# An S4D convolution and a token MLP on one core: the last four pieces of the inverse transform taken from SBUF, with a small selection table and moved loads

## The chip, the cores and the metric

One core of a Trainium2 chip. The metric is the device time of one execution in microseconds. The kernel before took 704.68 us (median of 3 runs, 703.97 to 706.22).

## What is computed

An adaLN block over x of 2048 tokens and 448 channels: a layer norm with modulation, a long convolution with an S4D kernel (done as an FFT of 4096 points), a second layer norm, and an MLP across the token axis.

```python
mod = (_silu(c) @ w_mod).reshape(c.shape[0], 6, 1, -1)
sa, ca, ga, sb, cb, gb = (mod[:, k] for k in range(6))
h = _layernorm(x, axis=-1) * (1 + ca) + sa
x = x + ga * _A_ref(h, ...)        # y = irfft(rfft(h) * rfft(K)) + h * D_skip, K from the S4D parameters
h = _layernorm(x, axis=-1) * (1 + cb) + sb
x = x + gb * _B_ref(h, ...)        # layernorm over channels, then across tokens: (gelu(h^T w1 + b1) w2 + b2)^T
```

## The kernel before

The order of the instructions of PE (TensorE), DVE (VectorE), ACT (ScalarE) and POOL (GpSimd) is that of the code; the transfers stand in SP's queue in the order of the code too, and a transfer that waits holds up all that are behind it in that queue. SP waits ahead of each transfer for the one issued eight before it, as there are eight counters in turn.

The work has three parts. The first generates the convolution's kernel and the transforms of kernel and input. The second multiplies the two spectra and transforms back. It goes by 32 *pieces*: piece n is a pair of frequency rows (p = n mod 16) of one half of the channels (c = n div 16, DC = 224 channels each). Pieces 0 to 15 run beside the first part; pieces 16 to 31 run in the loop `for m in range(NP, 2 * NP + 2, 2)` (NP = 16), two in each round. A piece is

- `pc_load`: the input's spectrum `u` from DRAM (224 KB)
- `pc_s2`: eight matmuls `kx` on PE for the kernel's spectrum
- `pc_mul`: two products `zx`, `zy` on DVE, then two sums `z` on the engines that it is given (POOL, or DVE for the last piece)
- `pc_inv`: eight matmuls `vv`
- `pc_out`: two copies on ACT into `vt` (four buffers), and a transfer of it (224 KB) to `v_d` in DRAM

In round m PE does `kx` of m and m + 1, and then `vv` of m - 2 and m - 1.

The third part reads the rows of `v_d` back by token blocks r (16 blocks of 128 tokens; `ln_load`, 448 KB), finishes the inverse transform with the table `ft` (`ln_y`), adds x (`x_pair` loads two blocks of it, 2 x 224 KB), applies the layer norms (`y_sum`, `ln_mod`, `ln_out`) and feeds the MLP, whose weights a `WeightStream` loads (`wst.load`, 448 KB each time), rounds on ACT (`whi`) and corrects on DVE (`wlo`). The MLP's matmuls write `acc` and later `o`.

Blocks 0 and 1 don't wait for all of `v_d`. Their channel half 0 is loaded early (`ln_first`); half 1 is loaded for the pieces that are already out (`ln_second`), and the products of the latest pieces come from their `vt` in SBUF (`fresh_vt`): the table `fl` selects from such a `vt` the rows of block r with their factors, in matmuls of 128 x 128 by 128 x 224 (`ln_direct`), and `ln_main` adds the loaded rows. In the kernel before, these are the last two pieces, `fl` is a full table of 512 KB from DRAM, and `ln_main` takes 112 rows.

Of the kernel before, what the change touches and what calls it, by code (L numbers as in the profile page):

```python
# [11 lines left out]
F32 = mybir.dt.float32  # L12
# [9 lines left out]
L, D, N, F = 2048, 448, 256, 1792  # L22
P = 128
# [9 lines left out]
NP = 16  # L33
# [6 lines left out]
def dft_tables():  # L40
    n1 = np.arange(32)
    k1 = np.arange(32)
    n2 = np.arange(64)
    k2 = np.arange(64)
    nn = 4096
    t = {}
    w = 2 * np.pi * np.outer(n1, k1) / 64
    w1 = np.zeros((2, 32, 32))
    w1[0] = np.cos(w)
    w1[1] = -np.sin(w)  # L50
    w1[0, :, 0] = 1
    w1[1, :, 0] = (-1.0) ** n1
    wc = np.zeros((4, 32, 2, 4, 32))
    for g in range(4):
        for c in range(2):
            wc[g, :, c, g, :] = w1[c]
    wu = np.zeros((2, 2, 32, 32, 2, 2))
    for a in range(2):
        wu[:, a, ..., a] = w1.transpose(1, 2, 0)
    t["WU"] = wu.reshape(P, P)  # L60

    t["WC"] = wc.reshape(P, 2, 2, 2, 32).swapaxes(3, 4).reshape(P, 2 * P)
    s = np.zeros((2, 64, 32, 2, 64))
    i1 = np.zeros((2, 64, 32, 2, 64))
    i2 = np.zeros((2, 64, 32, 2, 64))

    def inverse(rows, cols, k, m, ang):
        a = np.cos(ang) * 2 / nn
        b = np.sin(ang) * 2 / nn
        i1[0, rows, k, m[0]] = a  # L70
        i1[1, rows, k, m[0]] = -b
        i2[1, rows, k, m[0]] = -a
        i2[0, rows, k, m[0]] = -b
        if len(m) > 1:
            i1[0, rows, k, m[1]] = b
            i1[1, rows, k, m[1]] = a
            i2[1, rows, k, m[1]] = -b
            i2[0, rows, k, m[1]] = a

    for k in range(1, 32):  # L80
        ang = 2 * np.pi * np.outer(n2, k + 64 * k2) / nn
        s[0, :, k, 0] = np.cos(ang)
        s[1, :, k, 0] = np.sin(ang)
        s[0, :, k, 1] = -np.sin(ang)
        s[1, :, k, 1] = np.cos(ang)
        inverse(slice(None), None, k, (0, 1), ang.T)


    for q in range(32):
        ang = 2 * np.pi * n2 * (32 + 64 * q) / nn  # L90
        s[1, :, 0, 0, q] = np.cos(ang)
        s[1, :, 0, 1, q] = -np.sin(ang)
        inverse(q, None, 0, (1,), ang)
    for q in range(33, 64):
        ang = 2 * np.pi * n2 * (64 * (q - 32)) / nn
        s[0, :, 0, 0, q] = np.cos(ang)
        s[0, :, 0, 1, q] = -np.sin(ang)
        inverse(q, None, 0, (0,), ang)
    s[0, :, 0, 0, 32] = 1
    s[0, :, 0, 1, 32] = (-1.0) ** n2  # L100
    i1[0, 32, 0, 0] = 1 / nn
    i2[1, 32, 0, 0] = (-1.0) ** n2 / nn
    s2 = s.reshape(P, 32 * P)

    su = s.swapaxes(3, 4).reshape(2, 64, 32, P)
    t["S2"] = su.reshape(2, 2, 2, 16, 32 * P).swapaxes(1, 2).reshape(P, 32 * P)

    one = np.einsum("cnk,cqkm->km", w1, su)
    t["SV"] = one[ones_k1()].T

    order = lambda a: a.reshape(P, 32, 2, 2, 2, 16).swapaxes(3, 4).reshape(2, 64, 32, P)
    v1, v2 = order(i1), order(i2)
    pairs = v1.reshape(2, 64, NP, 2, P).transpose(3, 1, 2, 0, 4).reshape(P, NP, 2 * P)
    t["SI"] = np.concatenate([s2.reshape(P, NP, 2 * P), pairs], 2).reshape(P, NP * 4 * P)
    t0 = np.zeros((P, 2, P))
    t0[32, 0] = v1[0, 32, 0] + v2[1, 32, 0]
    t0[:, 1] = pairs[:, 0, P:]
    t["T0"] = t0.reshape(P, 2 * P)
    ft = np.zeros((32, 2, 2, 32, 2))
    w = 2 * np.pi * np.outer(k1, n1) / 64  # L120
    f0 = np.cos(w)
    f1 = -np.sin(w)
    f0[0] = 1
    f1[0] = (-1.0) ** n1
    for h in range(2):
        ft[:, 0, h, :, h] = f0
        ft[:, 1, h, :, h] = f1
    t["FT"] = ft.reshape(P, 64)

    fl = np.zeros((2, 2, 2, 16, 2, 4, 2, 32, 2))  # L130
    for r in range(2):
        for g in range(2):
            fl[:, :, g, r, r, :, g] = ft[28:].transpose(1, 2, 0, 3, 4)
    t["FL"] = fl.reshape(P, 8 * P)


    te = np.zeros((3, 64, 16, 32))
    tg = np.zeros((3, 16, 4, 16, 32))
    n = np.arange(32)
    for d in range(16):  # L140
        te[0, 2 * d : 2 * d + 2, d] = 2 * n + 1
        te[2, 2 * d : 2 * d + 2, d] = -n
        tg[0, d, 0:2, d] = n
        tg[0, d, 2:4, d] = 1
        tg[2, d, 0:2, d] = -64 * n
        tg[2, d, 2:4, d] = 1
    tg = tg.reshape(3, 16, 2, 2, 512).swapaxes(1, 2)
    tt = np.concatenate([te.reshape(3, 64, 512), tg.reshape(3, 64, 512)], 1)
    tt[1] = -tt[0]
    t["TT"] = tt.reshape(3, P, 512)  # L150
    return {k: np.ascontiguousarray(v.astype(np.float32)) for k, v in t.items()}
# [74 lines left out]
def tile_adaln_s4d_mixer(ctx, tc, i, out):  # L226
    nc = tc.nc
# [19 lines left out]
    with ExitStack() as es:  # L247
# [514 lines left out]
        def pc_tables(n):  # L762

            real, h = pt[n][0], P // 2
            if n == NP:
                pt[n] = real, t0[:, 1]
                return
            imag = fp.tile([P, P], F32, tag="bt", name="bt", bufs=3)
            S.activation(imag[:, 0:h], real[:, h:P], AF.Copy, scale=-1.0)
            S.copy(imag[:, h:P], real[:, 0:h])  # L770
            pt[n] = real, imag
# [36 lines left out]
        def pc_out(n):  # L808
            c, p = divmod(n, NP)
            vt = swp.tile([P, 2, DC], F32, tag="vt", name="vt", bufs=4) if c else fp.tile([P, 2, DC], F32, tag="vt", name="vt")  # L810
            for k, v in enumerate(pv.pop(n)):
                S.copy(vt[:, k], v)  # L812
            if n >= 2 * NP - 2:
                fresh_vt.append(vt)
            rows = v_d[2 * p : 2 * p + 2, :, c * DC : (c + 1) * DC]
            nc.sync.dma_start(rows.rearrange("k p d -> p k d"), vt)
# [343 lines left out]
        def x_pair(r):  # L1160
            for g in range(2):
                nc.sync.dma_start(
                    xts[r // 2][64 * g : 64 * g + 64].rearrange("p r d -> p (r d)"), token_pair(x, r, g)
                )

        swp = es.enter_context(tc.tile_pool(name="swp", bufs=2, reuse_waits="tile"))
        fl = swp.tile([P, 2, 4, P], F32, name="fl", bufs=1)
        v_v = v_d.rearrange("k (ch g r) d -> r (k ch) g d", ch=4, g=2)
        vts, hs, sa, sb = {}, {}, {}, {}

# [10 lines left out]
        def ln_second(r, n):  # L1181
            nc.sync.dma_start(vts[r][0:n, :, DC : 2 * DC], v_v[r, 0:n, :, DC : 2 * DC])
# [35 lines left out]
        def ln_main(r, y):  # L1218
            vt = vts.pop(r)
            for g in range(2):  # L1220
                c1 = slice(DC, 2 * DC)
                T.matmul(y[64 * g : 64 * g + 64, c1], ft[0:112], vt[0:112, g, c1], start=False, stop=True)

        def ln_mod(r):
            mean, rs = sa.pop(r)
# [8 lines left out]
        def ln_out(r):  # L1234
# [12 lines left out]
            S.copy(h3h[:, r], h)  # L1247
            return lambda: V.tensor_tensor(h3l[:, r], h, h3h[:, r].bitcast(F32), ALU.subtract)

        last = ExitStack()  # L1250
        last.enter_context(tc.manual_schedule(engines={ENG.SP}))
        for n in (NP + 3, NP + 4):
            pc_load(n)
        pc_keep(NP - 1)
        pc_tables(NP)
        for m in range(NP, 2 * NP + 2, 2):

            if m < 2 * NP:
                for n in (m, m + 1):
                    pc_s2(n)  # L1260
                for n in (m, m + 1):
                    pc_mul(n, *([V, V] if n == 2 * NP - 1 else [G, G]))
                    if n + 1 < 2 * NP:
                        pc_tables(n + 1)
                    if n + 5 < 2 * NP:
                        pc_load(n + 5)
            if m > NP:
                for n in (m - 2, m - 1):
                    pc_inv(n)
                for n in (m - 2, m - 1):  # L1270
                    pc_out(n)
                    if m == 2 * NP and n == m - 2:
                        ln_second(0, 112)
                        ln_second(1, 112)
            if m == NP + 2:
                nc.sync.dma_start(fl, i["FL"].rearrange("p (r j m) -> p r j m", r=2, j=4))
            elif m in (NP + 4, NP + 6):
                ln_first((m - NP - 4) // 2)
            if m in (NP + 6, 2 * NP - 8):
                wst.load()  # L1280
            elif m == 2 * NP - 4:
                x_pair(0)

        S.activation(eps_t, eps_t, AF.Sqrt)
        V.memset(eps_t, EPS)
# [3 lines left out]
        wst.load()  # L1289
        wst.ahead(1, V, False)  # L1290
        part = wst.begin(2)
        ya_ = py.tile([P, D], F32, tag="y", name="y")
        yb_ = pms.tile([P, D], F32, tag="ms", name="y")
        ln_direct(0, ya_, range(4))
        ln_main(0, ya_)
        ln_direct(1, yb_, range(4))
        ln_main(1, yb_)
        y_sum(0, ya_)()
        ln_load(4)
# [129 lines left out]
```

## Time and profile before

| | |
|---|---|
| median of the runs shown | 704.68 us |
| the profiled execution | 708.53 us, span 706.3 us |
| busy share of the span | PE 88%, DVE 64%, ACT 62%, POOL 38% |
| pieces 16 to 31 on PE | about 370.6 to 404.6 us |
| first matmul of the MLP (`acc`, L1326) | 415.20 us |
| `fl<-in_FL_dram` | one transfer of 512 KB, issued at 379.54 us |

Times in rows are microseconds from the span's start. A row of the engines' timeline has start, length, engine, line, operation, what is written from what, how many, and in brackets the idle time of the engine ahead of it and what ended it. "SPq" is SP's queue of transfers, and a length there is that of the issue, not of the transfer.

### The profile page before, as it was taken

What the parts mean: (1) busy time and instruction counts of PE and PEld (TensorE: products, weight loads), DVE (VectorE), ACT (ScalarE), POOL (GpSimd) and SP (SyncE); (2) the same over time, 40 slices, a digit from 0 to 9 for tenths busy, and PEclk for the clock granted to TensorE, in tenths of its full rate; (3) what the DMA queues carried; (4) which work ended last, traced back from release to release, by engine and by line L of the source; (5) the groups of instructions that cost most, each with busy time, mean ns of one, the idle gap of its engine ahead of it and who ended that gap; (6) DMA issues with size and microseconds to landing.
All of it is one profiled execution on the core that took longest, in us unless ns stands there. A gap on an engine that the chain in (4) does not pass through costs nothing. (4 is left out here: it accounts for less than half of the span.)

```text
span 706.3 us, 18230 instructions
## 1 busy us (share of the span) xinstructions
PE 620.9 (88%) x7164; PEld 461.2 (65%) x7164; DVE 453.7 (64%) x877; ACT 438.6 (62%) x876; POOL 271.5 (38%) x326
## 2 busy tenths in 40 slices
PE   0659878889988779798989779999999999999997
PEld 0335445545534556565566647778999999999996
DVE  7469799889679468595866368777622263344441
ACT  5937698888877699998964458888422242222220
POOL 6486548449358768988776300000000000000000
PEclk9968999999998789999899989999999999999999
DMA  7695464468795425444247989984674445555540
GB/s 172 205 192 136 159 216 163 163 219 257 228 301 174 153 73 140 142 131 140 82 118 220 277 226 250 245 202 125 188 226 141 143 128 159 157 156 157 170 131 27
DMA packets 104051, 121.69 MB, mean 172 GB/s; under 512 B 12730, under 2 KB 91758, under 8 KB 103838
## 3 DMA queue, kind: packets, MB, share of 16 engines
q1 hardware_dynamic: 102430, 113.66, 56.1%
q0 software_dynamic: 1536, 6.87, 4.4%
q8 instruction: 57, 0.93, 0.6%
q14 instruction: 28, 0.23, 0.1%
HBM read 85.14 MB, written 34.87 MB: 170 GB/s over the span
## 5 line engine op out<-in xcount | busy, mean ns | idle before, releaser
L211 ACT CAST whi<-w 128x896 fp32r<-128x896 f32 x64 | 59.8, 939 | 135.5 <-PE o L1396 84.7
L655 POOL TENSOR_TENSOR G<-mag,gs 128x512 f32<-128x512 f32 x56 | 72.0, 1286 | 77.7 <-ACT gs L651 77.6
L220 DVE TENSOR_TENSOR wlo<-w,whi 128x896 fp32r<-128x896 f32 x64 | 68.1, 1087 | 40.3 <-ACT whi L211 31.0
L603 PE MATMUL xg<-tab,lph 64*128 64x512 f32 x112 | 66.3, 594 | 21.1 <-issue 7.9
L1326 PE MATMUL acc<-h3h,whi 128*128 128x448 f32 x224 | 83.7, 374 | 0.7 <-ACT h3h L1241 0.7
L1327 PE MATMUL acc<-h3l,whi 128*128 128x448 f32 x224 | 82.3, 368 | 0.0
L686 PEld LDWEIGHTS kg<-E,G 128*32 128x32 f32 x3584 | 59.0, 118 | 35.6 <-issue 16.3
L1328 PE MATMUL acc<-h3h,wlo 128*128 128x448 f32 x224 | 81.5, 364 | 0.0
L1396 PE MATMUL o<-ul,whi 128*128 128x448 f32 x224 | 81.3, 363 | 0.0
L1395 PE MATMUL o<-uh,whi 128*128 128x448 f32 x224 | 81.2, 362 | 0.0
L1397 PE MATMUL o<-uh,wlo 128*128 128x448 f32 x224 | 80.7, 360 | 0.0
L686 PE MATMUL kg<-E,G 128*32 128x64 f32 x3584 | 69.4, 233 | 6.1 <-issue 4.9
L603 PE MATMUL xe<-tab,lph 64*128 64x512 f32 x112 | 65.5, 588 | 10.1 <-ACT gs L652 7.5
L656 POOL TENSOR_TENSOR G<-mag,gs 128x512 f32<-128x512 f32 x56 | 71.9, 1283 | 0.0
L1399 DVE SCALAR_TENSOR_TENSOR y<-o,b,mod 128x448 f32<-128x448 f32 x16 | 10.9, 684 | 80.3 <-PE o L1397 80.3
L632 POOL TENSOR_TENSOR m<-mag,w 128x512 f32<-128x512 f32 x56 | 59.7, 1067 | 6.0 <-DVE E L663 1.5
L657 DVE TENSOR_TENSOR E<-m,xe 128x512 f32<-128x512 f32 x56 | 38.1, 680 | 30.0 <-ACT xe L650 24.0
L640 ACT ACTIVATE ab<-xe 128x512 f32<-128x512 f32 x56 | 34.0, 606 | 31.7 <-PE xe L603 16.6
L1326 PEld LDWEIGHTS acc<-h3h,whi 128*128 128x128 f32 x224 | 42.6, 190 | 14.3 <-issue 3.3
L603 PE MATMUL xe<-tab,lex 64*128 64x512 f32 x56 | 32.8, 598 | 19.4 <-DMA lex<-wm 17.3
L614 ACT ACTIVATE mag<-xe 128x512 f32<-128x512 f32 x56 | 35.5, 633 | 17.0 <-PE xe L603 6.6
L1328 PEld LDWEIGHTS acc<-h3h,wlo 128*128 128x128 f32 x224 | 42.5, 190 | 3.0
(235 smaller groups left out, 1471.6 us busy)
## 6 DMA issues: line engine op xcount, KB each, us to landing
w<-in_B_w_dram SPq DMA_DIRECT2D x64, 224.0 KB
w<-in_B_w_dram SPq DMA_DIRECT2D x32, 448.0 KB
yu_d<-yt SPq DMA_DIRECT2D x16, 448.0 KB
yi<-yu_d SPq DMA_DIRECT2D x16, 448.0 KB
us_d<-uo SPq DMA_DIRECT2D x16, 448.0 KB
u<-us_d SPq DMA_DIRECT2D x32, 224.0 KB
v_d<-vt SPq DMA_DIRECT2D x32, 224.0 KB
vt<-v_d SPq DMA_DIRECT2D x14, 448.0 KB
```

Of the source, the lines that this page charges most:

```text
L211: self.nc.scalar.copy(hi, w)
L220: eng.tensor_tensor(lo, w, hi.bitcast(F32), ALU.subtract)
L603: T.matmul(out[k], lhs[r], rhs[r], start=start, stop=stop)
L655: G.tensor_tensor(Gt[:, 1], mg_, v32(sg), ALU.mult)
L656: G.tensor_tensor(Gt[:, 0], mg_, v32(cg_), ALU.mult)
L686: T.matmul(kgs[g][32 * q : 32 * q + 32, m], Gt[:, c, d], E[:, c, d], start=h == 0 and c == 0 and m == 0, stop=h == 1 and c == 1, skip_grou ...
L1326: nc.tensor.matmul(acc[f], hi[:, fs], h3h[:, r], start=r == 0, stop=False)
L1327: nc.tensor.matmul(acc[f], hi[:, fs], h3l[:, r], start=False, stop=False)
L1328: nc.tensor.matmul(acc[f], lo[:, fs], h3h[:, r], start=False, stop=r == 15)
L1395: nc.tensor.matmul(o, hi[:, ks], uh[kh][:, k], start=kh == 0 and k == 0, stop=False)
L1396: nc.tensor.matmul(o, hi[:, ks], ul[kh][:, k], start=False, stop=False)
L1397: nc.tensor.matmul(o, lo[:, ks], uh[kh][:, k], start=False, stop=kh == 1 and k == 6)
```

## The change

The table `FL` in DRAM shrinks from 128 x 1024 to 4 x 512 numbers (8 KB). `fl` in SBUF grows to eight 128 x 128 tables for each of the two blocks; DVE sets it to zero, and four transfers of 8 KB put the factors in place (`fl_rows`). The last four pieces are kept for blocks 0 and 1 instead of the last two; `ln_second` and `ln_main` go down to 96 rows, and `ln_second` is issued a round earlier. Block 0's products with pieces 28 and 29 stand ahead of `vv` of pieces 30 and 31. z of piece 16 is summed on DVE. The first two weight loads and the first `x_pair` change their places in SP's queue.

```diff
-    fl = np.zeros((2, 2, 2, 16, 2, 4, 2, 32, 2))
-    for r in range(2):
-        for g in range(2):
-            fl[:, :, g, r, r, :, g] = ft[28:].transpose(1, 2, 0, 3, 4)
-    t["FL"] = fl.reshape(P, 8 * P)
+    t["FL"] = ft[24:].transpose(1, 2, 0, 3, 4).reshape(4, 8 * 64)
...
-            if n >= 2 * NP - 2:
+            if n >= 2 * NP - 4:
                 fresh_vt.append(vt)
...
-        fl = swp.tile([P, 2, 4, P], F32, name="fl", bufs=1)
+        fl = swp.tile([P, 2, 8, P], F32, name="fl", bufs=1)
...
-                T.matmul(y[64 * g : 64 * g + 64, c1], ft[0:112], vt[0:112, g, c1], start=False, stop=True)
+                T.matmul(y[64 * g : 64 * g + 64, c1], ft[0:96], vt[0:96, g, c1], start=False, stop=True)
...
+        def fl_rows():
+
+            V.memset(fl, 0.0)
+            for r in range(2):
+                for g in range(2):
+                    p = 16 * g + r
+                    to = fl[p : p + 97 : 32, r, :, 64 * g : 64 * g + 64]
+                    nc.sync.dma_start(to, i["FL"].rearrange("p (j m) -> p j m", m=64))
+
...
         pc_tables(NP)
+        fl_rows()
         for m in range(NP, 2 * NP + 2, 2):
...
-                    pc_mul(n, *([V, V] if n == 2 * NP - 1 else [G, G]))
+                    pc_mul(n, *([V, V] if n in (NP, 2 * NP - 1) else [G, G]))
...
             if m > NP:
+                if m == 2 * NP:
+                    ya_ = py.tile([P, D], F32, tag="y", name="y")
+                    ln_direct(0, ya_, range(4))
                 for n in (m - 2, m - 1):
                     pc_inv(n)
                 for n in (m - 2, m - 1):
                     pc_out(n)
-                    if m == 2 * NP and n == m - 2:
-                        ln_second(0, 112)
-                        ln_second(1, 112)
-            if m == NP + 2:
-                nc.sync.dma_start(fl, i["FL"].rearrange("p (r j m) -> p r j m", r=2, j=4))
+                if m == 2 * NP - 2:
+                    ln_second(0, 96)
+                    ln_second(1, 96)
+            if m in (NP, 2 * NP - 4):
+                wst.load()
+            elif m == NP + 2:
+                x_pair(0)
             elif m in (NP + 4, NP + 6):
                 ln_first((m - NP - 4) // 2)
-            if m in (NP + 6, 2 * NP - 8):
-                wst.load()
-            elif m == 2 * NP - 4:
-                x_pair(0)
...
-        ya_ = py.tile([P, D], F32, tag="y", name="y")
         yb_ = pms.tile([P, D], F32, tag="ms", name="y")
-        ln_direct(0, ya_, range(4))
+        ln_direct(0, ya_, range(4, 8))
         ln_main(0, ya_)
-        ln_direct(1, yb_, range(4))
+        ln_direct(1, yb_, range(8))
```

PE's rows from the last `kx` (pieces 30 and 31) to the first matmul of the MLP, before. `vv` rows are `pc_inv`, two rows for each piece; L1214 and L1216 are `ln_direct` (`ft` on channel half 0, `fl` on the kept pieces), L1222 is `ln_main`, L1206 is `ln_y` of block 2:

```order
L806 MATMUL vv<-z,yk_1130 128x224 x2
L806 MATMUL vv<-z,bt 128x224 x2
L806 MATMUL vv<-z,yk_1130 128x224 x2
L806 MATMUL vv<-z,bt 128x224 x2
L1214 MATMUL y<-vt,ft 64x224 x2
L1216 MATMUL y<-vt,fl 128x224 x4
L1222 MATMUL y<-vt,ft 64x224 x2
L1214 MATMUL y<-vt,ft 64x224 x2
L1216 MATMUL y<-vt,fl 128x224 x4
L1222 MATMUL y<-vt,ft 64x224 x2
L1206 MATMUL y<-vt,ft 64x448 x2
L1326 MATMUL acc<-h3h,whi 128x448
```

and after:

```order
L1210 MATMUL y<-vt,ft 64x224 x2
L1212 MATMUL y<-vt,fl 128x224 x4
L802 MATMUL vv<-z,yk_1130 128x224 x2
L802 MATMUL vv<-z,bt 128x224 x2
L802 MATMUL vv<-z,yk_1130 128x224 x2
L802 MATMUL vv<-z,bt 128x224 x2
L1212 MATMUL y<-vt,fl 128x224 x4
L1218 MATMUL y<-vt,ft 64x224 x2
L1210 MATMUL y<-vt,ft 64x224 x2
L1212 MATMUL y<-vt,fl 128x224 x8
L1218 MATMUL y<-vt,ft 64x224 x2
L1202 MATMUL y<-vt,ft 64x448 x2
```

One group of four `fl` products with the `ft` ones now stands between `vv` of 28 and 29 and `vv` of 30 and 31; block 1 has eight `fl` products in a row.

SP's queue from the transfer out of piece 15 to the transfers out of pieces 28 and later, before (`u` is `pc_load`, `v_d<-vt` is `pc_out`, `w` a weight load, `xt` an `x_pair`, L1179 `ln_first`, L1182 `ln_second`, L1173 `ln_load`):

```order
L816 DMA v_d<-vt 128x2x224
L749 DMA u<-us_d 128x448 x4
L816 DMA v_d<-vt 128x2x224 x2
L1276 DMA fl<-in_FL_dram 128x1024
L749 DMA u<-us_d 128x448 x2
L816 DMA v_d<-vt 128x2x224 x2
L1179 DMA vt<-v_d 128x2x224
L749 DMA u<-us_d 128x448 x2
L816 DMA v_d<-vt 128x2x224 x2
L1179 DMA vt<-v_d 128x2x224
L191 DMA w<-in_B_w_dram 64x1x896 x2
```

...and on from there, to the first full `ln_load`:

```order
L191 DMA w<-in_B_w_dram 64x1x896 x2
L749 DMA u<-us_d 128x448
L816 DMA v_d<-vt 128x2x224 x4
L1162 DMA xt_6025<-in_A_u_dram 64x1x896 x2
L816 DMA v_d<-vt 128x2x224 x3
L1182 DMA vt<-v_d 112x2x224 x2
L816 DMA v_d<-vt 128x2x224
L1173 DMA vt<-v_d 128x2x448 x2
```

and after, the same two parts:

```order
L1253 DMA fl<-in_FL_dram 4x8x64 x2
L812 DMA v_d<-vt 128x2x224
L1253 DMA fl<-in_FL_dram 4x8x64 x2
L745 DMA u<-us_d 128x448 x2
L187 DMA w<-in_B_w_dram 64x1x896 x2
L745 DMA u<-us_d 128x448 x2
L812 DMA v_d<-vt 128x2x224 x2
L1158 DMA xt_6025<-in_A_u_dram 64x1x896 x2
```

```order
L812 DMA v_d<-vt 128x2x224 x2
L745 DMA u<-us_d 128x448
L812 DMA v_d<-vt 128x2x224 x4
L187 DMA w<-in_B_w_dram 64x1x896 x2
L812 DMA v_d<-vt 128x2x224 x2
L1178 DMA vt<-v_d 96x2x224 x2
L812 DMA v_d<-vt 128x2x224 x2
L1169 DMA vt<-v_d 128x2x448 x2
```

The 512 KB of `fl` are gone and four small transfers stand on either side of the `v_d` of piece 15. The first weight load moved up among the first `u`, the `xt` pair to where `fl` was, the second weight load down behind the `v_d` of pieces 24 to 27. `ln_second` (L1178 now) stands ahead of the last two `v_d` instead of ahead of the last one.

DVE's rows at the start of the loop, after (the first `zx`, `zy` here is piece 16):

```order
L701 TENSOR_TENSOR ks<-ks,dsk 128x4
L1248 MEMSET fl 128x2048
L785 TENSOR_TENSOR zx<-kx,u 128x448
L785 TENSOR_TENSOR zy<-kx,u 128x448
L787 TENSOR_TENSOR z<-zx,zy 128x224
L788 TENSOR_TENSOR z<-zx,zy 128x224
L785 TENSOR_TENSOR zx<-kx,u 128x448
L785 TENSOR_TENSOR zy<-kx,u 128x448
```

The memset is new, and so are the two `z` rows; both stand between rows that were neighbours before.

## The prediction

> **What bounds the kernel now.** I read the page first, then the busy time by stretches around the place of the change, then the chain of waits there, then each engine's rows in order of time. The profiled execution took 708.53 us, 2.2 us more than its span:
>
> ```profile
> span 706.3 us, 18230 instructions
> ```
>
> The stretches: each row has the five engines' busy time, the granted TensorE clock, the share of the DMA engines and GB/s.
>
> ```profile
> core 0: us, PE busy (x) PEld busy (x) DVE busy (x) ACT busy (x) POOL busy (x), PEclk, DMA share, GB/s
> 371.00:380.00 9.00, 8.85 (x82) 5.88 (x76) 6.18 (x11) 2.69 (x15) 5.61 (x9) 1.00 0.49 135
> 380.00:394.00 14.00, 14.00 (x134) 10.32 (x134) 8.66 (x16) 7.57 (x34) 10.90 (x18) 1.00 1.02 296
> 394.00:404.50 10.50, 6.68 (x49) 5.27 (x45) 4.06 (x8) 3.54 (x14) 2.51 (x4) 0.84 1.01 300
> 404.50:415.20 10.70, 6.50 (x38) 3.97 (x37) 5.94 (x17) 6.62 (x13) 0.00 (x0) 0.97 0.65 197
> 415.20:421.70 6.50, 6.50 (x16) 4.06 (x16) 3.10 (x11) 3.17 (x9) 0.00 (x0) 0.52 1.05 247
> 421.70:470.00 48.30, 48.30 (x229) 37.01 (x228) 39.38 (x119) 40.38 (x88) 0.00 (x0) 1.00 1.06 247
> 470.00:703.00 233.00, 231.70 (x1154) 214.09 (x1153) 100.76 (x158) 72.22 (x101) 0.00 (x0) 1.00 0.52 147
> ```
>
> From 421.70 to 703 PE is never idle to speak of (48.30 of 48.30, 231.70 of 233.00), at full clock. The token MLP there is a block of fixed length, so what counts is when it starts: the end moves with the first `acc` matmul at 415.20. In front of it stand the second half of the convolution's pieces (16 to 31, up to 404.5) and the first layer norm (404.5 to 415.2). In 380 to 394 PE is full, but so is DMA (1.02); in 394 to 404.5 DMA is still full (1.01) and PE works 6.68 of 10.50 us at 0.84 of its clock. That is where time is lost. The chain of waits in that part (start, length, what):
>
> ```profile
> 381.68 6.49 DMA v_d<-vt
> ...
> 388.19 6.66 DMA w<-in_B_w_dram
> ...
> 394.91 5.62 DMA v_d<-vt
> ```
>
> Each step is a transfer of 5.6 to 6.7 us, and the second of them is a weight load, not the pieces' own data. PE's rows, with the idle time ahead and its end in brackets:
>
> ```profile
> 391.90 0.65 PE L806 MATMUL vv<-z,yk 64*128 64x224 f32 x4
> ...
> 393.62 1.73 PE L780 MATMUL kx<-yk,yk 128*64 128x224 f32 x16
> 396.95 0.80 PE L806 MATMUL vv<-z,yk 64*128 64x224 f32 x4 [1.60 <-ACT vt L812]
> ...
> 401.10 1.27 PE L806 MATMUL vv<-z,yk 64*128 64x224 f32 x4 [2.21 <-ACT vt L812]
> ...
> 403.47 1.09 PE L806 MATMUL vv<-z,bt 64*128 64x224 f32 x4
> 404.49 0.60 PE L1214 MATMUL y<-vt,ft 128*64 128x224 f32 x4
> 405.02 1.78 PE L1216 MATMUL y<-vt,fl 128*128 128x224 f32 x8
> 408.40 0.60 PE L1222 MATMUL y<-vt,ft 112*64 112x224 f32 x4 [1.59 <-DMA vt<-v_d]
> ...
> 415.20 0.74 PE L1326 MATMUL acc<-h3h,whi 128*128 128x448 f32 x1 [0.74 <-ACT h3h L1241]
> ```
>
> Sixteen `vv` matmuls take 393.62 - 391.90 = 1.72 us undisturbed. Those of pieces 28 and 29 (396.95) come after 1.60 us of idle time, those of 30 and 31 (401.10) after 2.21 us, and the latter need 3.46 us (to 403.47 + 1.09 = 404.56): half the clock. Both waits name ACT, which had waited itself:
>
> ```profile
> 396.46 1.31 ACT L812 COPY vt<-vv 128x224 f32<-128x224 f32 x4 [2.28 <-DMA v_d<-vt]
> ...
> 400.61 1.24 ACT L812 COPY vt<-vv 128x224 f32<-128x224 f32 x4 [2.00 <-DMA v_d<-vt]
> ...
> 404.50 0.59 ACT L812 COPY vt<-vv 128x224 f32<-128x224 f32 x2 [0.90 <-ACT vt L812]
> ...
> 406.51 1.76 ACT L211 CAST whi<-w 128x896 fp32r<-128x896 f32 x2
> ```
>
> At 396.46 and 400.61 ACT could not copy a product out, since the transfer out of an older `vt` (four buffers) had not landed. DVE and SP waited for the same traffic:
>
> ```profile
> 371.68 0.62 DVE L789 TENSOR_TENSOR zx<-kx,u 128x448 f32<-128x448 f32 x1 [3.95 <-issue]
> ...
> 395.32 0.62 DVE L789 TENSOR_TENSOR zx<-kx,u 128x448 f32<-128x448 f32 x1 [2.84 <-DMA u<-us_d]
> ...
> 399.98 0.62 DVE L789 TENSOR_TENSOR zx<-kx,u 128x448 f32<-128x448 f32 x1 [2.45 <-DMA u<-us_d]
> ...
> 401.17 0.39 DVE L791 TENSOR_TENSOR z<-zx,zy 128x224 f32<-128x224 f32 x1
> ...
> 407.47 1.09 DVE L220 TENSOR_TENSOR wlo<-w,whi 128x896 fp32r<-128x896 f32 x1 [0.74 <-ACT whi L211]
> 409.04 0.62 DVE L1199 SCALAR_TENSOR_TENSOR xt<-xt,y 128x448 f32<-128x448 f32 x1 [0.48 <-PE y L1222]
> ```
>
> ```profile
> 371.08 0.37 SPq L816 DMA_DIRECT2D v_d<-vt  x1
> 372.87 5.59 SPq L749 DMA_DIRECT2D u<-us_d  x4
> ...
> 379.54 0.50 SPq L1276 DMA_DIRECT2D fl<-in_FL_dram  x1
> ...
> 394.91 3.24 SPq L816 DMA_DIRECT2D v_d<-vt  x4
> ...
> 405.30 1.28 SPq L1182 DMA_DIRECT2D vt<-v_d  x2
> ...
> 409.57 1.68 SPq L1173 DMA_DIRECT2D vt<-v_d  x2
> ```
>
> `u` came late at 395.32 (2.84 us) and 399.98 (2.45 us). SP issued four `v_d` transfers only at 394.91, where the weight load of the chain had landed. So pieces 26 to 31 are bound by a DMA backlog that builds up from 380 on, where `fl` (512 KB, issued 379.54), two weight loads and the first x pair share the engines with `u` and `v_d`.
>
> **The change part by part.**
>
> *Traffic.* `fl` falls from 512 KB to four transfers of 8 KB. The first weight load (2 x 224 KB) goes ahead of 380, the x pair (448 KB) takes the place in the queue where `fl` stood, and the second weight load takes the place of the x pair. So 0.524 + 0.459 = 0.983 MB leave the stretch 380 to 404.5. It moved 14.0 x 296 + 10.5 x 300 GB/s = 7.29 MB; at about 298 GB/s the removed part is 3.3 us. What is more, of the 1.44 MB that stood ahead of the `v_d` of pieces 24 and 25 only the x pair is left. The moved weight load meets a share of 0.49 in 371 to 380, so some 4.6 us of DMA time are free there, and it needs 1.5 us: I cost it at nothing. If that cover were gone, it would cost that 1.5 us at 380.
>
> Is PE then fast enough to be the bound? A pair of pieces takes PE 1.7 us of `kx` (the 1.73 of 393.62) and 1.7 of `vv`, 3.4 us, and moves 4 x 224 KB = 0.918 MB of `u` and `v_d`, 3.1 us at 298 GB/s. So what is left of the backlog shrinks by 0.3 us a pair instead of growing; I expect the two stalls to go, and what comes next is PE's own pace.
>
> *PE from 393.62.* Before, `kx` of 30 and 31 to the end of `vv` takes 404.56 - 393.62 = 10.94 us. After: `kx` 1.7, `vv` 28 and 29 1.7, then what is newly put ahead of the last pieces: four `ft` matmuls (405.02 - 404.49 = 0.53 us) and four on `fl`. Eight on `fl` stand in 1.78 us with the drain, so four are 0.8 us; the last two need the copy of 29, which follows its product by about 0.7 us (two copies at 0.3), so the four end about 1.1 us after `vv` 29. Then `vv` 30 and 31 at 1.7 us. The `ft` ones lie beside the copies. Sum 1.7 + 1.7 + 1.1 + 1.7 = 6.2, gain 10.94 - 6.2 = 4.7 us. Counted the other way, 1.60 + 2.21 us of waiting and 1.7 us of half clock, less 1.1 us for the products, give 4.4; I keep 4.7 and leave the 0.3 to the range.
>
> *From the last copy to `acc`.* This is a chain of latencies: ACT's copy (404.50), the table load, the two weight casts (406.51), DVE's `wlo` (407.47), then `xt` (409.04), 6.16 us of layer norm, `acc` at 415.20. Only one wait in it goes: at 409.04 DVE had waited 0.48 us for `y`, because PE waited 1.59 us for the second half of `vt` (408.40, issued 405.30). That load now stands in the queue ahead of the last two `v_d` and reads 96 rows, so it no longer waits for pieces 28 to 30. It is issued behind the `v_d` of 29, about 398.5, and with the 3.1 us of 405.30 to 408.40 lands near 401.6; `y` is ready by 402.3, DVE about 403.8. Gain 0.5 us. The added `fl` matmuls (eight more, 1.6 us) otherwise lie in PE's idle time in 404.5 to 415.2 (6.50 of 10.70 us busy). The last `v_d` no longer stand behind that load, so the full `vt` loads (409.57) come at least as much earlier as `acc`.
>
> *The memset of `fl`* (128 x 2048) is new on DVE. The trace has smaller ones:
>
> ```profile
> L310 DVE MEMSET ones<- 128x512 bf16 x1 | 0.5, 485 | 0.1
> ...
> L1141 DVE MEMSET ft<- 128x64 f32 x1 | 0.1, 112 | 0.0
> ```
>
> (485 - 112)/448 = 0.83 ns per element, so 1.77 us; the upper end is a two-input operation, 0.62 us for 448 elements (371.68), or 2.8 us. It stands where DVE idled 3.95 us before 371.68, so both ends cost nothing. Behind it in SP's queue wait the first two small transfers, and behind these a `v_d` issued at 371.08: 367.73 + 1.77 = 369.5, plus two issues of 0.50 (379.54) gives 370.5. The other two fit before 372.87, where SP waits for DVE anyway. At 2.8 us that `v_d` is 0.5 us late, which nobody awaits.
>
> *Piece 16 multiplied on DVE instead of POOL.* A subtraction takes DVE 0.39 us (401.17) and POOL
>
> ```profile
> 367.84 0.66 POOL L791 TENSOR_TENSOR z<-zx,zy 128x224 f32<-128x224 f32 x1 [2.37 <-DVE ks L705]
> ```
>
> so z of 16 is done 0.7 us sooner, and DVE's next `zx` 0.7 us later, and with it z of 17 by some 0.6 us. PE has short waits at either place there. I take 0, ends -0.5 and +0.5 us.
>
> Sum: 4.7 + 0.5 = 5.2 us. The first `acc` goes from 415.20 to 410.0, the span from 706.3 to 701.1, the profiled execution from 708.53 to 703.3. The median shown, 704.68, is 3.85 us under the profiled time; the same 5.2 us off gives 699.5.
>
> **The rivals.**
>
> *DMA stays the bound.* Then the stretch shortens by no more than its bytes: the `v_d` that landed at 400.53 lands 3.3 us earlier, at 397.2; copies, early products and `vv` follow to about 400.5 at full and 402.2 at half clock, against 404.56. With the 0.5 us that is 2.9 to 4.5 us, 701.0 on average. For it: a share of 1.01 with little slack (3.1 of 3.4 us a pair). Against: the 0.983 MB go in front of the place that stalls.
>
> *The memset holds up POOL.* POOL's z of piece 15 (the row at 367.84) runs at the same time, and PE stands behind it. Blocked for the memset's length it costs up to 1.77 us, 5.2 - 1.7 = 3.5: 701.2. No row here has a long memset beside POOL, so nothing excludes it. The Trainium skill, SBUF — State Buffer, section "Who interferes with whom", says that a VectorE instruction with at most one SBUF input outside the 2-port modes doesn't contend with GpSimd; no run here shows it, and by that rule this rival falls away.
>
> *The clock falls out otherwise.* In 415.20 to 421.70 the clock was 0.52: 6.5 us at half, 3.1 us of lost work. The 0.84 over 394 to 404.5 is 1.7 us lost, so that stretch at half was 3.4 us long. If the one at `acc` also lasts 3.4 us, 1.6 us more are won: 697.9. If it lasts 10 us, 1.6 are lost: 701.1. Which one an execution meets can't be read from one profile, so the sum keeps the length of before. The Trainium skill, TensorE: Matmul & The Clock Gate, section "What's actually happening", has the gate judged in free-running windows of about 3.4 us. By that rule the first matmuls after a long idle time run at half clock for one to two windows, as the phase has it; the lengths of 3.4 and 6.5 us here agree.
>
> *Slower.* The backlog stays as it was and the early products turn into a wait in front of PE: piece 29's copy ends at 401.8 (two after 400.61), then two products, then `vv` 30 and 31 at half clock to about 406.0 instead of 404.56; less the 0.48 us at 409.04 that is 1.0 us worse, 705.7. It is measurably slower only where that copy is later than about 402.9, which 0.98 MB less traffic speaks against.
>
> **How the numbers follow.** About 0.3% (2.1 us) is what a measurement of this kernel can tell from no change. The forecast, 4.3 to 6.0 us won, has 0.58; DMA as the bound 0.17; POOL held up 0.05; the luckier clock 0.06. All these are faster by over 0.3%: 0.86. A gain under 2.1 us or the mild form of the slower rival: 0.10. Slower by more: 0.04. The range goes from 697.6 (luckier clock and 0.5 from piece 16, in part) to 702.5 (DMA as the bound at its poor end with the memset in part), 0.82 or so.
>
> **What would show it.** Right: no wait of ACT for `v_d` over 0.5 us and none of DVE for `u` over 1 us after 385; `vv` of 30 and 31 at full clock; the end of the last copy near 400.4 and `xt` near 403.8; first `acc` near 410. DMA share ahead of 380 up, and under 1 somewhere in 385 to 400. Wrong: `vt` copies that still wait for `v_d` (then DMA is the bound), PE waiting in front of the early `fl` products, z of piece 15 over 1.5 us late, or a PE that is idle after the first `acc`, because weights don't keep up with the earlier start.

## The result, and the profile after

The changed kernel took 696.71 us (median of 4 runs, 690.71 to 697.46) beside 704.33 us of the kernel before (4 runs, 699.08 to 706.22): ratio 0.9891, 95% interval 0.9847 to 0.9936. (Ratios and intervals here are those on record for the runs of a comparison; a ratio is not always exactly the quotient of the two medians beside it.) It is faster, as forecast, but 696.71 lies 0.9 us under the lower end of the range (697.6) and 2.8 us under the forecast. The profiled execution took 697.46 us:

```profile
span 695.5 us, 18257 instructions
```

Its stretches, cut at about the same points of the program as those of before (the cut at 388.20 is the start of `kx` of 30 and 31, that at 394.00 in before is 0.38 us behind it; five engines' busy time, granted clock, DMA share, GB/s):

```profile
365.70:374.70 9.00, 8.87 (x83) 6.02 (x78) 7.02 (x14) 2.68 (x15) 4.46 (x8) 1.00 0.66 170
374.70:388.20 13.50, 13.50 (x130) 9.97 (x128) 9.30 (x17) 7.16 (x32) 10.40 (x17) 1.00 1.06 348
388.20:395.50 7.30, 7.30 (x62) 5.56 (x60) 3.31 (x7) 3.32 (x14) 2.88 (x5) 1.00 0.88 263
395.50:405.80 10.30, 7.52 (x42) 5.29 (x40) 5.87 (x17) 6.64 (x14) 0.00 (x0) 1.00 0.64 195
405.80:412.30 6.50, 6.49 (x22) 4.67 (x23) 4.25 (x17) 4.10 (x11) 0.00 (x0) 0.74 1.06 254
460.00:692.00 232.00, 231.04 (x1151) 213.53 (x1149) 99.75 (x157) 71.63 (x99) 0.00 (x0) 1.00 0.52 147
```

The third row answers about to 394.00 to 404.50 of before: 7.30 us instead of 10.50, PE full instead of 6.68 busy, the clock 1.00 instead of 0.84, DMA at 0.88 instead of 1.01. The first row has the moved weight load (0.66 instead of 0.49 of DMA). PE's rows there, to the first `acc`:

```profile
388.20 1.74 PE L776 MATMUL kx<-yk,yk 128*64 128x224 f32 x16
389.87 0.65 PE L802 MATMUL vv<-z,yk 64*128 64x224 f32 x4
...
391.58 0.60 PE L1210 MATMUL y<-vt,ft 128*64 128x224 f32 x4
392.11 1.78 PE L1212 MATMUL y<-vt,fl 128*128 128x224 f32 x8
393.82 0.65 PE L802 MATMUL vv<-z,yk 64*128 64x224 f32 x4
...
395.06 0.54 PE L802 MATMUL vv<-z,bt 64*128 64x224 f32 x4
...
398.28 0.60 PE L1218 MATMUL y<-vt,ft 96*64 96x224 f32 x4 [0.96 <-DMA vt<-v_d]
...
405.81 0.71 PE L1332 MATMUL acc<-h3h,whi 128*128 128x448 f32 x1 [0.90 <-ACT h3h L1237]
```

No idle time stands in front of any `vv`. ACT's copies, three rows of DVE and three of SP's queue:

```profile
391.30 1.08 ACT L808 COPY vt<-vv 128x224 f32<-128x224 f32 x4
394.92 0.59 ACT L808 COPY vt<-vv 128x224 f32<-128x224 f32 x2 [2.55 <-issue]
395.68 0.59 ACT L808 COPY vt<-vv 128x224 f32<-128x224 f32 x2 [0.16 <-ACT vt L808]
...
397.69 1.76 ACT L207 CAST whi<-w 128x896 fp32r<-128x896 f32 x2
```

```profile
387.23 0.62 DVE L785 TENSOR_TENSOR zx<-kx,u 128x448 f32<-128x448 f32 x1 [0.16 <-DMA u<-us_d]
...
398.65 1.09 DVE L216 TENSOR_TENSOR wlo<-w,whi 128x896 fp32r<-128x896 f32 x1 [0.74 <-ACT whi L207]
399.66 0.61 DVE L1195 SCALAR_TENSOR_TENSOR xt<-xt,y 128x448 f32<-128x448 f32 x1
```

```profile
390.21 1.22 SPq L187 DMA_DIRECT2D w<-in_B_w_dram  x2
...
392.98 1.62 SPq L1178 DMA_DIRECT2D vt<-v_d  x2
...
399.98 1.22 SPq L1169 DMA_DIRECT2D vt<-v_d  x2
```

These rows show that the copies wait for nothing of DMA, that `u` is late once and by 0.16 us, and that DVE goes from `wlo` straight on to `xt`.

For the comparison of profiles the program is cut into six parts: to the first `kx` of piece 16; from there to the last `kx` row (pieces 30 and 31); to the end of the last `vv`; to DVE's first `xt` of the layer norm; to the first `acc`; and on to the `y` of block 5, behind which PE works without a break. From that `y` to the end of the span it is 277.1 to 277.6 us in every kernel.

| profile | piece 16 at | to last `kx` | to end of `vv` | to `xt` | to `acc` | to `y` of block 5 | piece 16 to there |
|---|---|---|---|---|---|---|---|
| before | 370.60 | 23.01 | 10.95 | 4.48 | 6.15 | 13.87 | 58.46 |
| after | 365.30 | 22.91 | 7.40 | 4.05 | 6.15 | 12.59 | 53.10 |

58.46 - 53.10 = 5.36 us are won in the part that the change touches. Of the spans' difference (706.3 - 695.5 = 10.8 us) another 5.30 us are in the first part, which the change does not touch. So two questions are open: what the 5.36 us consist of, and whether the 5.30 us belong to the change.

### The profile page after: what moved, and what is told of

Read it like the earlier page. It is cut to its first block, busy times and chain, and to the rows that moved or that the text cites. A ratio compares the mean times of both kernels' runs of the same rounds, so it can differ in the third digit from the quotient of the medians.

```text
span 695.5 us, 18257 instructions
## 1 busy us (share of the span) xinstructions
PE 621.8 (89%) x7180; PEld 462.8 (67%) x7180; DVE 459.1 (66%) x880; ACT 438.2 (63%) x876; POOL 270.8 (39%) x324
```

## The experiments

**The two kernels once more, unedited.** 

> The kernel before, unchanged. Measured from the first kx matmul of piece 16 to the first acc matmul (44.6 us in the profile of before, 40.5 in that of the changed kernel), since the part ahead of it, which the change does not touch, differed by 5.3 us between the two profiles (370.6 and 365.3 us). Theory A (the changed stage gains about 4 us, the rest of the 7.6 us was the spread of the first part): the ratio is 1.000 within 0.004, the stage again 44 to 45.5 us, the first part anywhere from 364 to 372 us. Theory B (the change also makes the first part 3 to 5 us shorter by some side way): the first part is again about 370 us.

> The changed kernel, unchanged. Theory A: stage 40 to 41 us, first part anywhere from 364 to 372 us, ratio 0.992 to 0.995 (4 us of the stage, up to 1.5 us of clock at the first acc matmuls). Theory B: first part again about 365 us, ratio about 0.989.

These and the later runs were on three chips, each time with runs of the kernel before on the same chip. The kernel before against itself: 1.0007 (0.9983 to 1.0031). The changed one: 697.92 us against 702.53, 0.9920 (0.9889 to 0.9951). Piece 16 started at 365.99 us in this profile of before and at 367.16 in this one of after: the order of the first pair is turned round. The touched part took 59.35 and 53.41 us, 5.94 apart. So the first part's 5.30 us are not the change's.

**The traffic alone**: before, with the small table (four of the 128 x 128 tables a block) and the moved loads; two kept pieces, 112 rows and z of piece 16 on POOL stay.

```diff
-    if m == NP + 2: nc.sync.dma_start(fl, i["FL"]...)
-    if m in (NP + 6, 2 * NP - 8): wst.load()
-    elif m == 2 * NP - 4: x_pair(0)
+    fl_rows()                        # ahead of the loop
+    if m in (NP, 2 * NP - 4): wst.load()
+    elif m == NP + 2: x_pair(0)
```

> The kernel before with the small table (four tables a block, zeroed by DVE, four transfers of 4 KB) and with the weight loads and the x pair at their new places, but with two kept pieces, all their products behind the last piece, the load of 112 rows where it was, and z of piece 16 on POOL. If the gain is the traffic's alone: no stalls in front of the last four pieces, kx of 30 to the end of vv 5.3 to 5.6 us instead of 10.94, stage 39 to 40 us, as good as the changed kernel or 1 us better, ratio 0.990 to 0.994. If the two more pieces from SBUF are needed for it: waits of over 1 us for the load of 112 rows take their place, stage 41.5 us or more.

Measured: 699.27 us, 0.9957 (0.9928 to 0.9987); 5.51 us from the last `kx` to the end of `vv` instead of 10.95. No copy and no `vv` waits for DMA. But the next wait is longer:

```profile
390.84 0.60 PE L1210 MATMUL y<-vt,ft 128*64 128x224 f32 x4
391.37 1.78 PE L1212 MATMUL y<-vt,fl 128*128 128x224 f32 x8
396.06 1.01 PE L1218 MATMUL y<-vt,ft 112*64 112x224 f32 x4 [2.91 <-DMA vt<-v_d]
```

PE stands 2.91 us before the product with the 112 rows, because their load stands behind the `v_d` of piece 30 in SP's queue; `xt` comes 6.21 us after the last `vv`. The traffic takes away the stalls, and the kept pieces, with the load of the rows issued earlier, take away this wait (4.05 us in after). From piece 16 to the `y` of block 5 this kernel takes 54.26 us: of the 5.36 us of the first pair the traffic alone gives 4.20 in this profile, and the rest of the change 1.16 more. `acc` comes 40.90 us after piece 16, which is neither the 39 to 40 us nor the 41.5 us or more of the two expectations, and only 0.39 us later than in after.

**The products late**: after, with all of block 0's `fl` products behind the last piece.

```diff
-    if m == 2 * NP:
-        ya_ = py.tile([P, D], F32, tag="y", name="y")
-        ln_direct(0, ya_, range(4))
...
-    ln_direct(0, ya_, range(4, 8))
+    ya_ = py.tile([P, D], F32, tag="y", name="y")
+    ln_direct(0, ya_, range(8))
```

> The changed kernel with block 0's products with pieces 28 and 29 behind the last piece, together with the others. The forecast took 0.8 us for those four products; the profile shows 1.7 us for them and 0.5 us for the four ft ones, in front of the last two pieces. If that is a cost on the path: the last vv ends 1.8 to 2.2 us earlier, and since y then waits for its products and the 96-row load, the first acc comes 0.5 to 1 us earlier (stage 39.5 to 40 us). If the early products only fill a wait: no change of the stage (40.5 us) or a loss, since four more products then stand in front of y.

Measured: 697.37 us, 0.9909 (0.9880 to 0.9939). 5.51 us to the end of `vv`, 4.33 to `xt`, and `acc` 38.91 us after piece 16 instead of 40.51:

```profile
389.10 0.60 PE L1210 MATMUL y<-vt,ft 128*64 128x224 f32 x4
389.63 3.29 PE L1212 MATMUL y<-vt,fl 128*128 128x224 f32 x16
392.86 0.60 PE L1218 MATMUL y<-vt,ft 96*64 96x224 f32 x4
...
406.53 0.97 PE L1202 MATMUL y<-vt,ft 128*64 128x448 f32 x4 [0.83 <-DVE xt L1195]
...
408.82 0.47 PE L1331 MATMUL acc<-h3l,whi 128*128 128x448 f32 x1 [0.92 <-DVE h3l L1244]
```

So the early half of the products costs 1.89 us in front of `vv` and saves 0.28 behind it: there the table load, the casts and `wlo` run anyway. The 1.6 us at `acc` are more than was expected. Half of it is given back: PE is at full clock behind `acc` and waits for the layer norm, 0.83 and 0.92 us (the last two rows), so that the `y` of block 5 comes 0.82 us earlier (52.28 against 53.10).

**The small table alone, and the loads put back.** The first is before with `fl_rows()` in place of the 512 KB and all loads where they were; the second is after with the loads at the old places.

```diff
 # after, loads back
-    if m in (NP, 2 * NP - 4): wst.load()
-    elif m == NP + 2: x_pair(0)
+    if m in (NP + 6, 2 * NP - 8): wst.load()
+    elif m == 2 * NP - 4: x_pair(0)
```

> The kernel before with the small table alone: four tables a block zeroed by DVE and filled by four transfers of 4 KB; the weight loads and the x pair stay where they were, two kept pieces. Theory A (bytes decide): 0.52 of the 0.98 MB that left the stretch, so about half of what the traffic gained from kx of 30 to the end of vv (10.95 or 9.73 us before, 5.51 with all of the traffic's edits): 7.5 to 8.5 us. Theory B (the place in the queue decides, that is the weight loads ahead of the transfers out of pieces 24 and 25): the stalls stay, 9.5 us or more. Ratio 0.997 under A, 1.000 under B.

> The changed kernel with the two weight loads and the x pair put back to where they stood before; small table, four kept pieces, early products stay. Theory A: half of the traffic's relief is left, kx of 30 to the end of vv 9 to 10 us (7.40 in the changed kernel, of which 2.2 us are the early products), stage to the fifth block's y 2 us longer than the changed kernel's 53.1 to 53.4 us. Theory B: the stalls are back in full, 11 to 12 us, since the early products also wait behind them.

Measured: table alone 700.57 us, 0.9965 (0.9942 to 0.9988); loads back 699.22 us, 0.9943 (0.9910 to 0.9977). PE's rows with the stalls, of the table alone and then of the loads put back:

```profile
393.91 0.80 PE L802 MATMUL vv<-z,yk 64*128 64x224 f32 x4 [1.64 <-ACT vt L808]
...
397.18 0.80 PE L802 MATMUL vv<-z,yk 64*128 64x224 f32 x4 [1.33 <-ACT vt L808]
```

```profile
389.17 1.78 PE L1212 MATMUL y<-vt,fl 128*128 128x224 f32 x8 [1.27 <-ACT vt L808]
```

From the last `kx` to the end of `vv` it is 8.58 us with the table alone, against 10.95 and 9.73 in two profiles of before and 5.51 with the loads moved too. With the loads back it is 8.87, against 7.40 of after. So the small table without the moved loads leaves stalls, with two kept pieces (1.64 and 1.33 us) and with four (1.27); the moved loads take these away and are worth 3.07 us with two kept pieces, 1.47 with four. Both parts of the bytes count. The expected 7.5 to 8.5 us (table alone) and 9 to 10 us (loads back) were both missed by a little, the second on the good side, with the `y` of block 5 about 1 us later than in after and not 2; the bytes' share comes nearer than the stalls in full (9.5 us or more, 11 to 12 us). Why the moved loads are worth only half as much with four kept pieces was not tried, nor were the moved loads under the large table.

**x ahead**: the kernel with late products, with the second x pair and the next weights issued ahead of the full `vt` loads, since there DVE waited for x:

```profile
402.04 0.62 DVE L1195 SCALAR_TENSOR_TENSOR xt<-xt,y 128x448 f32<-128x448 f32 x1 [1.70 <-DMA xt<-in_A_u_dram]
```

```diff
+    x_pair(2)
+    wst.load()
     for r in (2, 3):
         ln_load(r, False)
```

> The kernel with all products late, and the x pair of blocks 2 and 3 and the third weight load issued ahead of the two full loads of v_d instead of behind them. Those two loads wait for the last transfer into v_d, and SP stands still for 3.1 us in that time (396.85 to 399.98 in the changed kernel); DVE then waited 0.92 us for that x pair. If that wait is what holds the first blocks of the layer norm: start of block 5's y 0.8 to 1.5 us earlier than the 52.28 us after kx of 16, ratio 0.987 to 0.990. If the load of block 2's v_d only lands later by the bytes put ahead of it: no change (52.3) or up to 1 us longer.

Measured: 697.81 us, 0.9920 (0.9894 to 0.9946), 52.92 us from piece 16 to block 5 against 52.28 without it (and 52.97 when that kernel was profiled again, below). So nothing is won. The wait has moved:

```profile
405.73 0.97 PE L1202 MATMUL y<-vt,ft 128*64 128x448 f32 x4 [1.98 <-DMA vt<-v_d]
```

The `y` of block 2 now waits for the full load instead of DVE for x. That the bytes behind the last piece are the limit, whatever their order, fits this but is not shown by one other order.

**Late products and the changed kernel again, and PE filled.** The last is after with eight extra matmuls (their product is read by nobody), meant for PE's idle time ahead of `acc`, to keep the clock up.

```diff
+    if t in (-1, 0):                 # ahead of ln_y(2), and of mlp1 of block 0
+        for _ in range(4):
+            nc.tensor.matmul(acc[6][0:64, 0:DC], ft, mod[4][:, 0:DC], start=True, stop=True)
```

> The kernel with all products late, once more, beside the changed kernel on the same chip. From the profiles (52.28 us from kx of 16 to block 5's y against 53.10 and 53.41) it should be 0.8 to 1.1 us faster than the changed kernel, 0.1 to 0.2%, which the runs can't tell; the stage should be 52.3 us again within 0.3. If the stage of the first look was luck: 53 us or more.

> The changed kernel, a third time. If the first comparison's 7.6 us was the spread of the first part (fewer runs), the ratio is again near 0.992 to 0.993, the stage to block 5's y 53.0 to 53.5 us, the rest 277.1 us. If the change has a further effect of 2 to 3 us somewhere else: 0.989.

> The changed kernel with eight more matmuls (64 x 224 of ft and mod, into an acc that is begun anew later): four ahead of block 2's y and four ahead of the first acc matmul, where PE idled 0.9 us each. They fill the clock gate's window, so the first acc matmuls should run at full clock. If half clock there costs time, as the rival of the prediction had it: 1.0 to 1.6 us less from the first acc to block 5's y (12.6 and 12.9 us in the changed kernel's profiles), ratio 0.990. If the layer norm of the first blocks sets the pace there: no change, PE waits for it instead (12.4 to 13.4 us).

Measured: late products 694.64 us, 0.9895 (0.9852 to 0.9937); changed kernel 697.65, 0.9936 (0.9905 to 0.9967); filled 697.10, 0.9924 (0.9889 to 0.9959), which can't be told from the changed kernel. The first block's MLP, of the filled kernel and then of after, is the stretch between the last two rows of each:

```profile
401.81 1.54 PE L1348 MATMUL acc<-mod,ft 128*64 128x224 f32 x7 [1.33 <-DVE xt L1195]
...
405.73 0.47 PE L1332 MATMUL acc<-h3h,whi 128*128 128x448 f32 x1
...
408.33 0.97 PE L1202 MATMUL y<-vt,ft 128*64 128x448 f32 x4
```

```profile
405.81 0.71 PE L1332 MATMUL acc<-h3h,whi 128*128 128x448 f32 x1 [0.90 <-ACT h3h L1237]
...
410.17 0.97 PE L1202 MATMUL y<-vt,ft 128*64 128x448 f32 x4
```

At full clock the same twelve matmuls take 2.60 us instead of 4.36, 1.76 us less. But the extra matmuls put `acc` 2.10 us later (42.61 after piece 16 instead of 40.51), and the `y` of block 5 comes at 53.43 instead of 53.10: the gain is paid for in front. The first row shows why: the first four extra matmuls did not fill the idle time. PE idled 1.33 us, for an `xt` as in after, and began them 38.69 us after piece 16, when `y` of block 2 starts in after (38.63), so that they pushed it back; the other four then stood ahead of `acc`. Nor does this show that they kept the clock up, since six of the eleven profiles without them are at full clock there too, as this first `acc` of the late products:

```profile
399.66 0.47 PE L1330 MATMUL acc<-h3h,whi 128*128 128x448 f32 x1
```

Of the expectations, the 1.0 to 1.6 us less from the first `acc` to block 5 came, and more (12.59 to 10.82), while the ratio, 0.9924 with its interval, can't tell 0.990 from the changed kernel's. The late products' second profile gave 52.97 us where 52.3 within 0.3 was expected.

All profiles, with the time ahead of piece 16 in which the granted clock was 0.5 ("half clock"):

| profile | half clock before the pieces | piece 16 at | last `kx` to `vv` end | to `xt` | piece 16 to `acc` | to `y` of block 5 |
|---|---|---|---|---|---|---|
| before | 64.9 | 370.60 | 10.95 | 4.48 | 44.59 | 58.46 |
| before again | 58.0 | 365.99 | 9.73 | 6.53 | 46.04 | 59.35 |
| after | 51.2 | 365.30 | 7.40 | 4.05 | 40.51 | 53.10 |
| after, second | 64.9 | 367.16 | 7.40 | 4.05 | 40.51 | 53.41 |
| after, third | 58.0 | 364.90 | 7.43 | 4.05 | 40.53 | 52.96 |
| traffic only | 47.8 | 362.39 | 5.51 | 6.21 | 40.90 | 54.26 |
| table only | 61.4 | 367.52 | 8.58 | 5.80 | 43.55 | 57.47 |
| loads back | 37.5 | 360.88 | 8.87 | 4.05 | 41.98 | 54.13 |
| products late | 37.5 | 360.75 | 5.51 | 4.33 | 38.91 | 52.28 |
| products late, again | 41.0 | 361.49 | 5.51 | 4.86 | 39.43 | 52.97 |
| x ahead | 47.8 | 366.11 | 5.51 | 5.13 | 40.52 | 52.92 |
| PE filled | 30.7 | 363.12 | 7.40 | 4.05 | 42.61 | 53.43 |

## Why the prediction was right and where it was wrong

**The base and the range failed, not the gain.** Three comparisons of the changed kernel give 0.9891, 0.9920 and 0.9936. In the last two, the changed kernel has a mean of 697.88 us (22 runs, standard deviation 2.46), and the kernel before, over all its 90 runs after the first comparison, one of 702.88 (2.43; by chip 702.98, 703.29 and 702.18, so that most of the spread is within a chip): 5.0 us, with about 1.2 either way, where 5.2 was forecast. This mean lies inside the range, by 0.3 us. The touched part alone gives 5.36 and 5.94 us in the two pairs of profiles, so that nothing of the 5.0 is left for the first part. The step that failed is the line "The median shown, 704.68 [...]; the same 5.2 us off gives 699.5", with a range from terms of the touched part alone: what the untouched first part moves from run to run was put at nothing. Single runs of before go from 696.73 to 708.11, so the median of the three shown was 1.8 us above the mean of 90, and that of the four runs of after 1.2 below the mean of its 22. The three runs shown lay within 2.25 us and hid this spread, and 0.3% as what a measurement can tell was too sure for so few of them. The stretch from the start to piece 16, in before, after, and after with the products late:

```profile
0.00:370.60 370.60, 297.96 (x5474) 180.28 (x5474) 285.58 (x541) 302.01 (x605) 252.46 (x296) 0.91 0.58 170
```

```profile
0.00:365.30 365.30, 298.97 (x5475) 180.97 (x5475) 290.30 (x542) 301.93 (x605) 253.04 (x296) 0.93 0.60 172
```

```profile
0.00:360.75 360.75, 292.26 (x5474) 177.22 (x5474) 290.21 (x542) 301.78 (x605) 253.10 (x296) 0.95 0.60 174
```

The same matmuls take 10 us more or less, with a lower clock in the longer ones. The prediction priced the clock behind `acc` and in the last pieces only, and gave a luckier one 0.06; over this part the spread is larger than either of these, and it belongs to the run, not to the kernel. The clock goes with it, but does not account for all of it (see the last section).

**Step by step, against piece 16.**

- *The stalls go*: right. No copy waits for `v_d`, `u` is late by 0.16 us at most, the last `vv` run at full clock (393.82 to 395.60), DMA falls to 0.88. The traffic alone shows that this term is the traffic's.
- *PE from the last `kx` to the end of `vv`*: 7.40 us, not 6.2, so 3.55 us won and not 4.7. `kx` (1.67) and both `vv` (1.71, 1.78) are as priced. The term that was mis-sized is "Eight on `fl` stand in 1.78 us [...], so four are 0.8 us": the profile's "x8" is four instructions, each shown as two, as the order of the same place (x4) says. (So it is with "eight matmuls" `kx` and `vv` of a piece ahead: in the code and in the order they are four.) Four take 1.71 us (392.11 to 393.82). The copies end at 392.38, as priced, but with `fl` at 1.71 us PE doesn't wait for them, so the `ft` ones ahead (0.53) are no longer hidden beside them: 2.24 in place of 1.1, which is 1.14 of the 1.20 us missed.
- *The wait for `y`*: 4.48 to 4.05, 0.43 of the 0.5 forecast. The load of 96 rows landed 2 us later than said (PE at 398.28, 33.0 after piece 16, instead of 31.0): it was issued when said, 27.7 after piece 16, but PE got its rows 5.3 us later and not 3.1. `xt` stands behind `wlo` and did not notice. That "the last `v_d` no longer stand behind that load" is wrong: both do, as the order of SP's queue after the change shows. The full loads came earlier all the same, at 34.7 after piece 16 instead of 39.0.
- *From `xt` to `acc`*: 6.15 and 6.15, as said.
- *The memset*: 1.76 us (1.77 said), and nothing lost: from piece 16 to the last `kx` it is 23.01 us in both profiles of before, without it, and in the traffic and table kernels, with one of half the size; 22.91 with the full one and z of piece 16 on DVE. POOL is not held up either: its two sums beside the memset take 0.66 and 0.67 us, as before (0.66). The rows of DVE and of POOL in after:

```profile
362.81 1.76 DVE L1248 MEMSET fl<- 128x2048 f32 x1 [0.37 <-DVE ks L701]
```

```profile
362.53 0.66 POOL L787 TENSOR_TENSOR z<-zx,zy 128x224 f32<-128x224 f32 x1 [1.46 <-DVE ks L701]
363.15 0.67 POOL L788 TENSOR_TENSOR z<-zx,zy 128x224 f32<-128x224 f32 x1
```

  The Trainium skill, SBUF — State Buffer, section "Who interferes with whom", says that a VectorE instruction with at most one SBUF input, outside the 2-port modes, doesn't contend with GpSimd; these rows agree.
- *z of piece 16 on DVE*: 0.10 us won (23.01 to 22.91); said 0.
- *Behind `acc`*: left out of the sum and kept as a rival, and 1.28 us were won there (13.87 to 12.59): PE runs without a break in both profiles, and this one had 3.4 us at half clock where that of before had over 6. In these two profiles this makes up for the 1.15 us too much in the other term. So the forecast gain came out near 5.36 by luck: one term was too large, and one that was left out made up for it.

**The rivals.** *DMA stays the bound* falls: the traffic alone leaves no stall in front of `vv`. *POOL held up* falls by the rows above. *The clock falls out otherwise* is true at `acc` in its mechanism: one half-clock stretch of 3.4 us costs 1.76 us of PE there. But where PE keeps its clock it can wait next (0.83 and 0.92 us for the layer norm with the products late). From `acc` to block 5 it is 12.14 to 13.92 us in the six unfilled profiles at full clock and 12.40 to 13.87 in the five at half clock, so it decides little between kernels. *Slower* falls.

**A better version.** With all products late the mean of 12 runs is 695.78 us (standard deviation 2.15), against 697.88 for the changed kernel: 2.1 us, with some 1.6 either way. The ratios to before overlap (0.9909 and 0.9895 against 0.9920 and 0.9936); in the touched part the first pair of profiles shows 0.82 us (52.28, 53.10), the last pair nothing (52.97, 52.96). So the version is as good at least, and its gain in the touched part of these profiles is at most about half of what the means show. That it is faster is likely and not settled. In its second profile `xt` is 0.53 us later behind `vv`, with PE waiting 0.46 us for the 96 rows; why these landed later was not tried.

## What to carry to other kernels

Before a blind time is put on a few runs, look how much of the span is outside the change and how far that part moves from run to run: here 360.8 to 370.6 us, twice the gain. Compare stretches from a fixed point of the program, not ends of spans. Count instructions in the order of the code before a duration of the profile is divided by its count, and ask whether work in the stage that bounds can run beside a chain of latencies a few us later: here the early products cost 1.89 us in front and saved 0.28 behind.

## What the runs showed of the hardware

The first part's length goes with the time that PE spent at half clock in it: 30.7 to 64.9 us in these twelve profiles, for lengths from 360.75 to 370.60 (correlation 0.85; some 0.2 us of span for each us at half clock). It is not the whole of it: the filled kernel has the least half clock and only the fifth shortest first part, and the first profile of before and the second of after have 64.9 us both and are 3.44 us apart. The stretches are 3.41 us or multiples of it (6.8, 10.2, 13.7), at other places in each run. The Trainium skill, TensorE: Matmul & The Clock Gate, section "What's actually happening", has the gate judged in free-running windows of about 3.4 us; the lengths agree with it, and that the same program meets them in other places each time is what free-running windows would do. No run here sets their phase, so that this is the cause stays open.

The time around the span fell from 2.23 us (708.53 - 706.3) to 1.96 (697.46 - 695.5), and is about 2.2 in the kernels with two kept pieces and 2.0 in those with four. What it depends on was not looked for.
